# Product tiles in two pairs and a scan state in two tiles, in a fused attention and state-space kernel

## The chip, the cores and the metric

The kernel runs on one core of a Trainium2 chip as one launch. The metric is the device time of that launch in microseconds (us), less is better. TensorE (PE) multiplies matrices, ScalarE (ACT) computes exponentials, VectorE (DVE) does elementwise work, GpSimd (POOL) almost nothing, and SyncE (SP) issues the transfers.

## The reference

Two branches read one input `x` (2048 positions, 512 channels) and are mixed by a gate per position:

```python
g = _sigmoid((x * gate_w).sum(-1, keepdims=True))
a = _A_ref(x, wqkv, wo)          # softmax attention, 32 heads of 16, full 2048 x 2048 scores
b = _B_ref(x, A_re, A_im, ...)   # state-space convolution, 128 complex modes per channel
return g * a + (1 - g) * b

# in _B_ref
P = exp((dt * A)[:, :, None] * l)                 # powers of each mode, l = 0..2047
K = einsum("dn,dnl,dn->dl", Cc, P, dB).real       # one kernel of length 2048 per channel
y = causal convolution of u with K (by FFT), + u * Dskip
```

## The kernel before

**Attention.** 32 blocks (four heads by 512 queries) of 16 key quads each; a quad is four score tiles of 128 keys by 512 queries, one per head. All 2048 tiles go three at a time through 683 groups. For a group `qk` puts three tiles into one of two PSUM buffers `SC0`, `SC1`; `ex` (L909) is one exponential on ScalarE over the group, into a ring `ET`; `pv` multiplies by the values and sums in `OA`. At a block's end `norm_a`, `norm_b`, `norm_c` transpose and divide on VectorE.

**Vector sets.** Some quads are computed on VectorE instead. A set is one quad; its four tiles are spread over four consecutive groups (`SHAPE`: two tiles for ScalarE, one for VectorE). `bits` (L945) turns each tile's scores into the bit pattern of an approximate power of two in `DZ`; `batch` (L956) makes two shifted copies (`DU`, then `DZ` again), and the three versions are multiplied with the values and two scaled copies of them (`VS0`, `VS1`, made behind the groups in `VSAT`). The exponential of such a group is two tiles wide, 128x1024.

**State space.** `params` computes the modes and their powers `L1` to `L48` and the factor `MU` of one chunk of 64 positions. `base` builds the first 16 powers of each channel block in `B16`. `table` (L1211) makes the power tables: for each of 8 pairs of channel blocks it copies the 16 powers into `PT` and multiplies them by the 16th, 32nd and 48th power. Each complex product is, for its real and its imaginary part, two products into `tt1` and `tt2` and one sum into `PT`, through the helper `tt` (L1006). `PT` then goes to memory (`ptd`). `kstage` makes convolution kernels from it, `sstage` (L1297 on) the states of 32 chunks in `SG0` and `SG1` (channels 0 to 255, 256 to 511), evicted at L1309. `scan` (L1317) runs over the chunks, for each half in turn: the state `G` (fp32, real and imaginary) is multiplied by `MU` into `s2` and `s3` (L1336, L1338), the chunk's own state is added to `s2` (L1341), both are summed into `G` (L1344), and `G` is rounded to bf16 back into `SG` (L1347), 30 steps a half. The y stage multiplies states by powers, evicts 32 units (L1420), and reads them back turned; the last additions (L1575) and an output matmul of four row blocks close the kernel.

**The order of work** is computed when the kernel is built. Every operation is recorded with a cost; `Sched` holds generators with priorities (`table` 2, `scan` 3, `sstage` 2), and between two exponentials it fills the engines with whatever is ready, by start time and then priority. Each engine then runs its recorded list in order, with semaphore waits for what an operation depends on, its own engine's earlier instructions included for VectorE. An operation that would have to wait a moment for its predecessor lets another ready one go first.

Whether a set is taken is decided in `decide` (L799), group by group, inside windows:

```python
plan["used"] = max(plan["used"], idle() - DVCAP)
if plan["set"] is None and clear(x) and idle() - plan["used"] >= dvq():
    plan["used"] += dvq()
```

`idle()` is the time in which the planner's own books have VectorE idle so far; `dvq()` is the price of a set in such idle time, by `DVQ` dependent on which stage is done; credit over `DVCAP` lapses. `WIN` lists windows in groups: first, last, how many `DZ`/`DU` buffers, and how many of the two lists of key quads may be taken. `SGAT` gives the groups behind which the S stage of each half may start; `BUP` is the priority of the two steps. `place` packs all SBUF tiles by their first and last use into the free space.

Of the kernel before, what the change touches and what calls it, by code (L numbers as in the profile page):

```python
# [2 lines left out]

# [10 lines left out]
P = 128  # L14
# [21 lines left out]
BARE = 1  # L36
NS = 15
SGH = 256
SGAT = (175, 315)
SMM = .058  # L40
YR = 4
DOV = .8
# [372 lines left out]
def declare(nc, es):  # L415
# [72 lines left out]
        sb(f"B16{k}", 2 * 128 * 16)  # L488

    sb("PT", 2 * 2 * CB * T)  # L490
    sb("tt1", 2 * CB * 16)
    sb("tt2", 2 * CB * 16)
    sb("Qt", 2 * 32 * 128)
    sb("Kst", 2 * 8 * P)

    sb("SG0", 33 * 2 * SGH)
    sb("SG1", 33 * 2 * SGH)
    sb("G", 2 * 256, FP32)
    for n in ("s2", "s3"):
        sb(n, 2 * 256, FP32)  # L500

# [24 lines left out]
def place(nc, bufs):  # L526

    base, end = (nc.sbuf_base + 31) // 32 * 32, nc.sbuf_usable_end
    sbs = [b for b in bufs.values() if b.kind == "sb" and b.first is not None]

    def fit(order):
        done, top = [], base
        for b in order:
            n = (b.nbytes() + 31) // 32 * 32
            busy = sorted((o.lo, o.hi) for o in done if o.first <= b.last + 1 and b.first <= o.last + 1)
            at = base
            for lo, hi in busy:
                if at + n <= lo:
                    break
                at = max(at, hi)  # L540
            b.lo, b.hi = at, at + n
            top = max(top, b.hi)
            done.append(b)
        return top

    best, seed = None, 1
    for k in range(400):
        def rank(b):
            nonlocal seed
            seed = (seed * 1103515245 + 12345) % 2 ** 31  # L550
            w = seed / 2 ** 31 * (0 if k < 2 else .8)
            return (-(b.last - b.first > 300) if k % 2 else 0, -b.nbytes() * (1 + w * 2) * (b.last - b.first + 20) ** (w if k >= 2 else 0))
        order = sorted(sbs, key=rank)
        top = fit(order)
        if best is None or top < best[0]:
            best = (top, order)
    k = 0
    while best[0] > end and k < 12000:
        k += 1
        order = list(best[1])  # L560
        for _ in range(1 + k % 3):
            seed = (seed * 1103515245 + 12345) % 2 ** 31
            b = order.pop(seed // 7 % len(order))
            seed = (seed * 1103515245 + 12345) % 2 ** 31
            order.insert(seed // 7 % (len(order) + 1), b)
        top = fit(order)
        if top <= best[0]:
            best = (top, order)
    assert best[0] <= end, (best[0] - end, live(sbs))
    fit(best[1])  # L570
# [41 lines left out]
def record(nc, p, B, ins):  # L612
# [597 lines left out]

    def table():  # L1211
        yield ("AFTER", "D48")
        t1, t2 = B["tt1"], B["tt2"]
        H10 = dv(1024, 2)
        for pb in range(NBLK // 2):
            qr, blks = pb // 2, (2 * pb, 2 * pb + 1)
            yield ("AFTER", f"base{qr}")
            if pb:
                yield ("AFTER", f"K{2 * pb - 2}")
                yield ("AFTER", f"K{2 * pb - 1}")  # L1220
            B16 = B[f"B16{qr}"]
            bk = [(B16, 0), (B16, (1, 0)), (B16, (1, 64))]
            d0, b0 = 2 * CB * pb, 2 * CB * (pb % 2) * 16
            W = [(PT, 0, blks[0]), (PT, 1, blks[1])]
            for i in range(2):
# [3 lines left out]
            for m in range(1, 4):  # L1229
                Dm = B[f"D{16 * m}.{qr}"]  # L1230
                for part in range(2):
                    for ti, xr, yr in ((t1, 0, part), (t2, 1, 1 - part)):
                        yield ("DVE", H10)
                        tt("DVE", lambda ti=ti: ti(0, [[16, 2 * CB], [2, 8], [1, 2]]),
                           lambda xr=xr, b0=b0, B16=B16: B16(xr * 2048 + b0, [[16, 2 * CB], [2, 8], [1, 2]]),
                           lambda yr=yr, d0=d0, Dm=Dm: Dm(yr * 2 * P + 2 * (d0 % P), [[2, 2 * CB], [0, 8], [1, 2]]), ALU.mult,
                           bk + [(Dm, 0)], [(ti, 0)], H10)
                    yield ("DVE", H10)
                    tt("DVE", lambda part=part, m=m: PT(part * CB * T + 16 * m, [[PTN, 2], [T, CB], [1, 16]]),
                       lambda: t1(0, [[CB * 16, 2], [16, CB], [1, 16]]), lambda: t2(0, [[CB * 16, 2], [16, CB], [1, 16]]),  # L1240
                       ALU.add if part else ALU.subtract, [(t1, 0), (t2, 0)], W, H10)
# [73 lines left out]


    def scan():  # L1317
        G, s2, s3 = B["G"], B["s2"], B["s3"]
        MU = B["MU"]
        e = "DVE"  # L1320

        W = [[256, 2], [1, 256]]

        def pair(h):
            sg, d0 = SG[h], 256 * h
            ks = [(sg, k, (h, 'S')) for k in range(32)]
            for k in range(8):
                yield ("AFTER", f"sg{8 * h + k}")
            for c in range(NCH - 1):
                so = 2 * SGH * (c + 1)  # L1330
                if c == 0:
                    yield (e, .34)
                    op(e, lambda v, so=so: v.tensor_copy(G(0, W), sg(so, [[SGH, 2], [1, 256]])), ks, [(G, 0)], c=.34)
                    continue
                yield (e, F5)
                op(e, lambda v: v.tensor_tensor(s2(0, W), G(0, W), MU(d0, [[0, 2], [1, 256]]), ALU.mult), key("G", "MU"), [(s2, 0)], c=F5)  # L1336
                yield (e, F5)
                op(e, lambda v: v.tensor_tensor(s3(0, W), G(256, [[-256, 2], [1, 256]]), MU(D + d0, [[D, 2], [1, 256]]), ALU.mult),  # L1338
                   key("G", "MU") + [(MU, 1)], [(s3, 0)], c=F5)
                yield (e, F5)  # L1340
                op(e, lambda v, so=so: v.tensor_tensor(s2(0, W), s2(0, W), sg(so, [[SGH, 2], [1, 256]]), ALU.add),  # L1341
                   [(s2, 0)] + ks, [(s2, 0)], c=F5)
                yield (e, F5)
                op(e, lambda v: v.tensor_tensor(G(0, [[1, 512]]), s2(0, [[1, 512]]), s3(0, [[1, 512]]), ALU.add),  # L1344
                   [(s2, 0), (s3, 0)], [(G, 0)], c=F5)
                yield (e, .34)
                op(e, lambda v, so=so: v.tensor_copy(sg(so, [[SGH, 2], [1, 256]]), G(0, W)), key("G"),  # L1347
                   ks if c < NCH - 2 else [(sg, k, (h, 'G')) for k in range(32)], c=.34)
# [35 lines left out]
    def ystage():  # L1384
        def unit(u):
# [14 lines left out]
            for q in range(4):  # L1400
                yield ("PE", .15)
                for ri in range(2):
                    for j in range(4):
                        i = 4 * q + 2 * (j % 2) + j // 2
                        mm(lambda q=q, j=j: MB(64 * q, [[1, 64]], 32 * j, 32),
                           lambda ri=ri, i=i: sg(ri * SGH + CB * k8 + 16 * hf + 8 * (i % 2) + i // 2, [[2 * SGH, 32]]),
                           lambda ri=ri, i=i: Py(r * YN + ri * 16 * T + i * T, [[1, T]]),
                           [(sg, b_, (h, 'G')) for b_ in range(32)] + [(sg, "z"), (Py, r, u)], ky, False, False,
                           pos=(0, 32 * j), c=.075 if j == 0 else 0, a=16, cfg="C")
            for q in range(4):  # L1410
                yield ("PE", .09)
# [406 lines left out]
```

## Time and profile before

| | us |
|---|---|
| median of three runs | 838.77 |
| the three runs | 838.77, 840.81, 838.6 |
| span of the profiled execution, first to last instruction | 837.7 |
| ScalarE busy | 819.1 (98%) |
| VectorE busy | 783.3 (94%) |
| TensorE matmuls busy | 698.3 (83%) |
| first exponential starts, last one starts | 11.6, 827.3 |
| first scan rounding, last scan rounding | 401.3, 689.6 |

The profiled execution's own time is its span of 837.7 us; the launch's time has about 1 us more around it. Sums are made against the span and carried over to the median by that difference. In the profile's rows a group of instructions has its count, then its busy time and the mean duration of one, then the idle time of its engine just before its members. Durations of neighbours overlap on VectorE and ScalarE, so a rate is read from starts or from busy time over count, and not from the mean duration.

### The profile page before, as it was taken

To read this page: it belongs to the slowest core of one execution; us is meant where nothing else is said; L and a number is where in the kernel's file an instruction comes from. 1 tells how busy PE (TensorE), PEld (TensorE's weight loads), DVE (VectorE), ACT (ScalarE), POOL (GpSimd) and SP (SyncE) were. 2 spreads that over 40 slices of the span, in tenths; PEclk is the share of its full clock that TensorE was granted. 3 is DMA by queue.
4 is the path that set the end of the run, shared out by engine and by line. 5 is a ranking of instruction groups with operands and counts; after the bars stand their busy time and mean duration, and the time that the engine had idled before them with its cause. 6 is when DMAs were issued, how large, how long until landed. Compare 5 with 4: busy or idle time off the path is not lost.

```text
span 837.7 us, 21043 instructions
## 1 busy us (share of the span) xinstructions
PE 698.3 (83%) x8982; PEld 253.4 (30%) x8982; DVE 783.3 (94%) x1344; ACT 819.1 (98%) x695; POOL 11.0 (1%) x13
## 2 busy tenths in 40 slices
PE   7877777787679888887788887788897779999996
PEld 3232332122122332332232332244342224333332
DVE  5799999999889998999999999999899999999996
ACT  7999999999999999999999999999999999999996
POOL 4000000000000000000000000000000000000000
PEclk9999999999999999999999999999999999999999
DMA  9650044792361976873392846045564414544113
GB/s 207 142 83 10 23 77 92 202 228 57 128 177 46 223 123 179 119 205 67 139 144 40 143 67 143 1 108 136 140 148 109 115 54 110 135 99 132 34 45 101
DMA packets 248465, 94.90 MB, mean 113 GB/s; under 512 B 223156, under 2 KB 235316, under 8 KB 246324
## 3 DMA queue, kind: packets, MB, share of 16 engines
q1 hardware_dynamic: 246500, 92.51, 49.6%
q8 instruction: 70, 1.15, 0.5%
q10 hardware_dynamic: 1872, 1.05, 0.5%
q14 instruction: 23, 0.19, 0.1%
HBM read 33.08 MB, written 35.01 MB: 81 GB/s over the span
## 4 chain that ended last, share of the span: by engine, by line
ACT 83%; DVE 7%; PE 5%; DMA 3%; SPq 0%; issue 0%; ACTq 0%; DVEq 0%
ACT ET L909 83%; PE SC L628 2%; PE OA L628 2%; DVE tt L1006 2%; DMA gm_ptd<-PT 2%; DVE PT L1006 1%; DMA Wk<-in_A_wqkv_dram 1%; DVE DZ L945 1%; PE MB L628 1%; DMA XY<-gm_xrd 1%; DVE DZ L956 0%; DVE s L1336 0%; DVE OT L980 0%; DVE s L1338 0%; SPq L1371 0%
## 5 line engine op out<-in xcount | busy, mean ns | idle before, releaser
L909 ACT ACTIVATE ET<-SC 128x1536 bf16<-128x1536 f32 (+1 forms) x683 | 810.8, 1537 | 5.9 <-PE SC L628 3.6
L628 PE MATMUL SC<-Qm,KT 32*128 32x512 bf16 x2048 | 276.1, 387 | 122.4 <-ACT ET L909 107.7
L628 PE MATMUL OA<-wm 128*32 128x512 bf16 (+3 forms) x1374 | 204.1, 365 | 1.2 <-DVE wm L681 1.2
L945 DVE TENSOR_SCALAR DZ<-SC 128x512 uint16<-128x512 f32 x256 | 170.1, 684 | 10.3 <-PE SC L628 9.4
L628 PE MATMUL OA<-ET,VE 128*32 128x512 bf16 x1792 | 179.7, 394 | 0.0
L628 PEld LDWEIGHTS SC<-Qm,KT 32*128 32x128 bf16 x2048 | 70.9, 91 | 339.8 <-ACT ET L909 303.1
L628 PEld LDWEIGHTS OA<-ET,VE 128*32 128x32 bf16 x1792 | 45.7, 93 | 102.0 <-issue 97.6
L628 PEld LDWEIGHTS OA<-wm 128*32 128x32 bf16 (+2 forms) x1374 | 54.6, 95 | 25.9 <-issue 17.7
L956 DVE TENSOR_SCALAR DZ<-DZ 128x2048 uint16<-128x2048 uint16 x64 | 43.8, 684 | 3.0 <-PE OA L628 2.7
L1309 DVE TENSOR_SCALAR SG<-MB 128x512 bf16<-128x512 f32 x64 | 43.7, 684 | 3.0 <-DMA gm_ptd<-PT 1.7
L956 DVE TENSOR_SCALAR DU<-DZ 128x2048 uint16<-128x2048 uint16 x64 | 43.1, 684 | 0.1
L628 PE MATMUL MB<-X,Qt 128*128 128x64 bf16 x512 | 42.1, 244 | 1.2 <-DVE SG L1309 1.2
L1344 DVE TENSOR_TENSOR G<-s,s 128x512 f32<-128x512 f32 x60 | 41.3, 688 | 1.1
L1338 DVE TENSOR_TENSOR s<-G,MU 128x512 f32<-128x512 f32 x60 | 41.1, 684 | 0.0
L1341 DVE TENSOR_TENSOR s<-s,SG 128x512 f32<-128x512 f32 x60 | 41.0, 683 | 0.0
L1336 DVE TENSOR_TENSOR s<-G,MU 128x512 f32<-128x512 f32 x60 | 40.9, 682 | 0.0
L628 PEld LDWEIGHTS MB<-X,Qt 128*128 128x128 bf16 x512 | 28.8, 116 | 20.0 <-issue 20.0
L1006 DVE TENSOR_TENSOR ft<-FP,L 128x1024 f32<-128x1024 f32 (+1 forms) x32 | 34.4, 1086 | 0.2
L1006 DVE TENSOR_TENSOR PT<-tt,tt 128x1024 bf16<-128x1024 bf16 x48 | 32.9, 685 | 0.5
L628 PEld LDWEIGHTS MB<-Py,SG 128*32 128x32 bf16 x1024 | 27.8, 168 | 6.8 <-issue 4.1
L628 PE MATMUL MB<-Py,SG 128*32 128x64 bf16 x1024 | 28.6, 231 | 0.0
L1347 DVE CAST SG<-G 128x512 bf16<-128x512 f32 x60 | 25.3, 422 | 1.1
(167 smaller groups left out, 613.9 us busy)
## 6 DMA issues: line engine op xcount, KB each, us to landing
gm_ptd<-PT SPq DMA_DIRECT2D x16, 1024.0 KB, 5.9
Py<-gm_ptd SPq DMA_DIRECT2D x32, 512.0 KB, 4.3
gm_kpd<-Kst SPq DMA_DIRECT2D x16, 256.0 KB, 3.1
Tt<-gm_kpd SPq DMA_DIRECT2D x128, 32.0 KB, 3.2
gm_xrd<-in_A_x_dram SPq DMA_DIRECT2D x1, 2048.0 KB, 13.7
gm_xcd<-wm SPq DMA_DIRECT2D x4, 512.0 KB, 10.4
gm_xcd<-XR SPq DMA_DIRECT2D x32, 64.0 KB, 1.9
Wo<-in_A_wo_dram SPq DMA_DIRECT2D x4, 512.0 KB, 3.8
```

Source lines behind the costliest of these rows:

```text
L628: op("PE", lambda t: t.matmul(out(), lhsT(), rhs(), start=start, stop=stop, skip_group_check=True, **kw), R, W, c=c, lat=.15, a=a, cfg=cfg)
L909: op("ACT", lambda a: a.activation(ET(512 * e, [[1, 512 * n]]), sc(0, [[1, 512 * n]]), AF.Exp, scale=DH ** -0.5), [(sc, i, g) for i in ran ...
L945: op("DVE", lambda v: v.tensor_scalar(z.u16(512 * k, [[1, 512 * n]]), sc(512 * na, [[1, 512 * n]]), XS, XB, ALU.mult, ALU.add), [(sc, na + ...
L956: op("DVE", lambda v: v.tensor_scalar(t.u16(0, [[1, 2048]]), z.u16(0, [[1, 2048]]), float(STEP[k][0]), None, ALU.add), R, W, c=.07 + 2048 ...
L1006: op(eng, lambda v: v.tensor_tensor(o(), a(), b_(), f), R, W, c=c)
L1309: op("DVE", lambda v, kh=kh, part=part: v.tensor_scalar(sg(2 * SGH + SGH * part + CB * k8 + 16 * kh, [[2 * SGH, 32], [1, 16]]), MB(0, [[16 ...
L1336: op(e, lambda v: v.tensor_tensor(s2(0, W), G(0, W), MU(d0, [[0, 2], [1, 256]]), ALU.mult), key("G", "MU"), [(s2, 0)], c=F5)
L1338: op(e, lambda v: v.tensor_tensor(s3(0, W), G(256, [[-256, 2], [1, 256]]), MU(D + d0, [[D, 2], [1, 256]]), ALU.mult), key("G", "MU") + [(M ...
L1341: op(e, lambda v, so=so: v.tensor_tensor(s2(0, W), s2(0, W), sg(so, [[SGH, 2], [1, 256]]), ALU.add), [(s2, 0)] + ks, [(s2, 0)], c=F5)
L1344: op(e, lambda v: v.tensor_tensor(G(0, [[1, 512]]), s2(0, [[1, 512]]), s3(0, [[1, 512]]), ALU.add), [(s2, 0), (s3, 0)], [(G, 0)], c=F5)
L1347: op(e, lambda v, so=so: v.tensor_copy(sg(so, [[SGH, 2], [1, 256]]), G(0, W)), key("G"), ks if c < NCH - 2 else [(sg, k, (h, 'G')) for k i ...
```

## The change

The table's products go into two pairs of tiles, used in turn, and the sum of product n is issued between the two products of n + 1. The scan's state alternates between two tiles, and the rounding of a step's state is issued in the next step, between that step's second and third sums; the y stage waits for the roundings by a name of their own for each chunk. The search that packs the tiles is another one, with new random moves. Six constants of the planner change.

```diff
-SGAT = (175, 315)
+SGAT = (227, 311)
-VSAT = (158, 500)
-WIN = ((170, 475, 2, 1), (475, 540, 3, 1), (540, 678, 4, 2))
-DVQ = (("scan1", 0.0), ("scan0", 0.5), ("S15", 1.0), (None, 0.5))
+VSAT = (138, 474)
+WIN = ((184, 482, 2, 1), (482, 540, 3, 1), (540, 678, 4, 2))
+DVQ = (('scan1', 0.25), ('scan0', 0.5), ('S15', 1.25), (None, 0.5))
 BP = 2.2
-DVCAP = 2.0
-BUP = 1
+DVCAP = 5.0
+BUP = 0
...
-    sb("tt1", 2 * CB * 16)
-    sb("tt2", 2 * CB * 16)
+    for n in ("tt10", "tt11", "tt20", "tt21"):
+        sb(n, 2 * CB * 16)
...
-    sb("G", 2 * 256, FP32)
+    for n in ("G0", "G1"):
+        sb(n, 2 * 256, FP32)
...
+            def product(n, ti, xr, qr=qr, B16=B16, b0=b0, d0=d0, bk=bk):
+                m, part = 1 + n // 2, n % 2
+                Dm, t, yr = B[f"D{16 * m}.{qr}"], B[f"tt{ti}{n % 2}"], (part, 1 - part)[xr]
+                tt("DVE", lambda: t(0, [[16, 2 * CB], [2, 8], [1, 2]]),
...
+            def total(n, W=W):
+                m, part = 1 + n // 2, n % 2
+                t1, t2 = B[f"tt1{n % 2}"], B[f"tt2{n % 2}"]
+                tt("DVE", lambda: PT(part * CB * T + 16 * m, [[PTN, 2], [T, CB], [1, 16]]),
...
+            for n in range(7):
+                if n < 6:
                     yield ("DVE", H10)
+                    product(n, 1, 0)
+                if n:
+                    yield ("DVE", H10)
+                    total(n - 1)
+                if n < 6:
+                    yield ("DVE", H10)
+                    product(n, 2, 1)
...
+        def cast(h, c):
+            sg, G = SG[h], B[f"G{c % 2}"]
+            op(e, lambda v: v.tensor_copy(sg(2 * SGH * (c + 1), [[SGH, 2], [1, 256]]), G(0, W)), [(G, 0)], [(sg, ("G", c), h)], c=.34)
...
+            for c in range(1, NCH - 1):
                 so = 2 * SGH * (c + 1)
...
+                G, H = B[f"G{1 - c % 2}"], B[f"G{c % 2}"]
...
+                if c > 1:
+                    yield (e, .34)
+                    cast(h, c - 1)
                 yield (e, F5)
...
+                op(e, lambda v, H=H: v.tensor_tensor(H(0, [[1, 512]]), s2(0, [[1, 512]]), s3(0, [[1, 512]]), ALU.add),
+                   [(s2, 0), (s3, 0)], [(H, 0)], c=F5)
+            yield (e, .34)
+            cast(h, NCH - 2)
```

More of the change, by code (lines that the diff above doesn't have):

```diff
@@ L529, in place @@
     sbs = [b for b in bufs.values() if b.kind == "sb" and b.first is not None]
+    n, cap = len(sbs), end - base
+    size = [(b.nbytes() + 31) // 32 * 32 for b in sbs]
+    near = [[j for j in range(n) if j != i and sbs[j].first <= sbs[i].last + 1 and sbs[i].first <= sbs[j].last + 1] for i in range(n)]
+    rnd = random.Random(1)
     def fit(order):
[L532 to L538, printed above, removed]
-                    break
[L540 to L569, printed above, removed]
@@ L570, in place @@
-    fit(best[1])
+        at = [-1] * n
+        for i in order:
+            x = 0
+            for lo, hi in sorted((at[j], at[j] + size[j]) for j in near[i] if at[j] >= 0):
+                if x + size[i] <= lo:
+                    break
+                x = max(x, hi)
+            at[i] = x
+        return at, sum(max(0, at[i] + size[i] - cap) for i in range(n))
+    keys = (lambda i: (-size[i], sbs[i].first - sbs[i].last), lambda i: -size[i] * (sbs[i].last - sbs[i].first + 20),
+            lambda i: (sbs[i].first + 300 > sbs[i].last, -size[i]))
@@ new lines, in place @@
+    order = min((sorted(range(n), key=key) for key in keys), key=lambda o: fit(o)[1])
+    at, cost = fit(order)
+    for k in range(30000):
+        if not cost:
+            break
+        bad = [i for i in range(n) if at[i] + size[i] > cap]
+        r = rnd.random()
+        i = rnd.choice(bad) if r < .6 else rnd.choice(near[rnd.choice(bad)]) if r < .8 else rnd.randrange(n)
+        new = list(order)
+        p = new.index(i)
+        new.pop(p)
+        new.insert(rnd.randrange(p + 1) if r < .6 else rnd.randrange(n), i)
+        a, c = fit(new)
+        if c <= cost or rnd.random() < math.exp((cost - c) / (2000 * max(.02, 1 - k / 30000))):
+            order, at, cost = new, a, c
@@ L571, in place @@
+    assert not cost, (cost, live(sbs))
+    for b, x in zip(sbs, at):
+        b.lo = base + x
+        b.hi = b.lo + (b.nbytes() + 31) // 32 * 32
     for b in sbs:
@@ L1228, in table @@
                                                                      B16(b0 + i * CB * 16, [[2048, 2], [16, CB], [1, 16]])), bk, [W[i]], c=.34)
[L1229 to L1237, printed above, removed]
-                    yield ("DVE", H10)
-                    tt("DVE", lambda part=part, m=m: PT(part * CB * T + 16 * m, [[PTN, 2], [T, CB], [1, 16]]),
-                       lambda: t1(0, [[CB * 16, 2], [16, CB], [1, 16]]), lambda: t2(0, [[CB * 16, 2], [16, CB], [1, 16]]),
-                       ALU.add if part else ALU.subtract, [(t1, 0), (t2, 0)], W, H10)
+            def product(n, ti, xr, qr=qr, B16=B16, b0=b0, d0=d0, bk=bk):
+                m, part = 1 + n // 2, n % 2
+                Dm, t, yr = B[f"D{16 * m}.{qr}"], B[f"tt{ti}{n % 2}"], (part, 1 - part)[xr]
+                tt("DVE", lambda: t(0, [[16, 2 * CB], [2, 8], [1, 2]]),
+                   lambda: B16(xr * 2048 + b0, [[16, 2 * CB], [2, 8], [1, 2]]),
+                   lambda: Dm(yr * 2 * P + 2 * (d0 % P), [[2, 2 * CB], [0, 8], [1, 2]]), ALU.mult, bk + [(Dm, 0)], [(t, 0)], H10)
@@ new lines, in total @@
+            def total(n, W=W):
+                m, part = 1 + n // 2, n % 2
+                t1, t2 = B[f"tt1{n % 2}"], B[f"tt2{n % 2}"]
+                tt("DVE", lambda: PT(part * CB * T + 16 * m, [[PTN, 2], [T, CB], [1, 16]]),
+                   lambda: t1(0, [[CB * 16, 2], [16, CB], [1, 16]]), lambda: t2(0, [[CB * 16, 2], [16, CB], [1, 16]]),
+                   ALU.add if part else ALU.subtract, [(t1, 0), (t2, 0)], W, H10)
+            for n in range(7):
+                if n < 6:
+                    yield ("DVE", H10)
+                    product(n, 1, 0)
[5 more added lines that the diff above has]
+                    product(n, 2, 1)
@@ L1342, in pair @@
                    [(s2, 0)] + ks, [(s2, 0)], c=F5)
+                if c > 1:
+                    yield (e, .34)
+                    cast(h, c - 1)
                 yield (e, F5)
[L1344 to L1348, printed above, removed]
+                op(e, lambda v, H=H: v.tensor_tensor(H(0, [[1, 512]]), s2(0, [[1, 512]]), s3(0, [[1, 512]]), ALU.add),
+                   [(s2, 0), (s3, 0)], [(H, 0)], c=F5)
+            yield (e, .34)
+            cast(h, NCH - 2)
             sch.mark(f"scan{h}")
@@ L1407, in unit @@
                            lambda ri=ri, i=i: Py(r * YN + ri * 16 * T + i * T, [[1, T]]),
[L1408 removed]
+                           [(sg, ("G", c), h) for c in range(1, NCH - 1)] + [(sg, k, (h, 'S')) for k in range(32)] + [(sg, "z"), (Py, r, u)], ky, False, False,
                            pos=(0, 32 * j), c=.075 if j == 0 else 0, a=16, cfg="C")
```

16 lines of the change are left out of this document (6 added, 10 removed).

## The prediction

> **What bounds the kernel now.** The page's engine shares come first, then the ScalarE groups kept apart by shape, then busy time by stage.
>
> ```profile
> span 837.7 us, 21043 instructions
> PE 698.3 (83%) x8982; PEld 253.4 (30%) x8982; DVE 783.3 (94%) x1344; ACT 819.1 (98%) x695; POOL 11.0 (1%) x13
> ACT 83%; DVE 7%; PE 5%; DMA 3%; SPq 0%; issue 0%; ACTq 0%; DVEq 0%
> L909 ACT ACTIVATE ET<-SC 128x1536 bf16<-128x1536 f32 x426 | 582.8, 1756 | 1.9 <-PE SC L628 1.6
> L909 ACT ACTIVATE ET<-SC 128x1024 bf16<-128x1024 f32 x257 | 248.4, 1175 | 3.9 <-PE SC L628 2.0 <-PE OA L628 1.6
> 241.60:690.00 448.40, 375.46 (x4974) 136.68 (x4970) 432.73 (x754) 445.29 (x375) 1.05 (x2) 0.99 0.55 120
> 690.00:828.70 138.70, 129.12 (x2087) 50.82 (x2087) 130.05 (x223) 137.02 (x140) 0.00 (x0) 1.00 0.39 95
> 828.70:837.70 9.00, 4.24 (x24) 1.50 (x20) 3.72 (x8) 1.17 (x2) 0.00 (x0) 0.92 0.18 59
> ```
>
> ScalarE is busy for 98% of the span and holds 83% of the chain that ended last. Its 683 exponentials (426 of three score tiles, 257 of two) are the work. In the stage rows the columns are PE, weight load, DVE, ACT, POOL. ScalarE idles 1.7 us of the last full stage and the closing tail is 9.0 us. So nothing shortens this kernel unless tiles leave ScalarE or its gaps go. Tiles leave by the vector sets: a set takes four tiles of one key quad, one from each of four groups, and computes them on VectorE. The 257 short groups are 64 sets (and one group at the end). VectorE is the second engine at the limit, 94%. What the change does to VectorE therefore reaches the end only through the number of sets, and I price a set first.
>
> On ScalarE a long group occupies 582.8 / 426 = 1.37 us, a short one 248.4 / 257 = 0.97 us: a set saves 4 x 0.40 = 1.6 us. On VectorE a set is four conversions (L945) and two steps (L956). Their starts, in a stretch where nothing waits, give the price:
>
> ```profile
> 329.24 1.92 DVE L945 TENSOR_SCALAR DZ<-SC 128x512 uint16<-128x512 f32 x3
> 331.08 0.68 DVE L956 TENSOR_SCALAR DU<-DZ 128x2048 uint16<-128x2048 uint16 x1
> 331.68 0.69 DVE L945 TENSOR_SCALAR DZ<-SC 128x512 uint16<-128x512 f32 x1
> 332.29 0.68 DVE L956 TENSOR_SCALAR DZ<-DZ 128x2048 uint16<-128x2048 uint16 x1
> 332.89 0.69 DVE L956 TENSOR_SCALAR DU<-DZ 128x2048 uint16<-128x2048 uint16 x1
> ```
>
> Each lasts 0.68 us, yet the next starts 0.60 us after it: neighbours overlap by 0.08. A set costs 6 x 0.60 = 3.6 us of VectorE. So 3.6 us freed on VectorE are worth at most 1.6 us at the end, 0.44 for one.
>
> **The change, part by part.** The instruction counts stay: a table pair still has 12 products and 6 sums, a scan step still 4 sums or products and one rounding. Only order and buffers change, so the saving is in the waits between neighbours. First the scan, in a stretch where other work hardly comes between:
>
> ```profile
> 526.36 0.43 DVE L1347 CAST SG<-G 128x512 bf16<-128x512 f32 x1
> 526.70 0.69 DVE L1336 TENSOR_TENSOR s<-G,MU 128x512 f32<-128x512 f32 x1
> 527.30 0.69 DVE L1338 TENSOR_TENSOR s<-G,MU 128x512 f32<-128x512 f32 x1
> 527.90 0.69 DVE L1341 TENSOR_TENSOR s<-s,SG 128x512 f32<-128x512 f32 x1
> 528.62 0.69 DVE L1344 TENSOR_TENSOR G<-s,s 128x512 f32<-128x512 f32 x1
> 529.35 0.43 DVE L1347 CAST SG<-G 128x512 bf16<-128x512 f32 x1
> 529.69 0.68 DVE L1336 TENSOR_TENSOR s<-G,MU 128x512 f32<-128x512 f32 x1
> L1344 DVE TENSOR_TENSOR G<-s,s 128x512 f32<-128x512 f32 x60 | 41.3, 688 | 1.1
> L1347 DVE CAST SG<-G 128x512 bf16<-128x512 f32 x60 | 25.3, 422 | 1.1
> L1341 DVE TENSOR_TENSOR s<-s,SG 128x512 f32<-128x512 f32 x60 | 41.0, 683 | 0.0
> ```
>
> The products start 0.60 apart (526.70, 527.30, 527.90). The sum L1344 reads what the instruction right in front of it wrote and starts 0.72 later (528.62); the rounding L1347 reads that sum and starts 0.73 later (529.35). A dependent neighbour costs 0.12 us. L1341, which depends on the instruction two in front, has no idle time and pays nothing. Most of the 0.12 hides as lost overlap: the rows show only 0.03 to 0.04 of it as idle, so the 1.1 us before L1344 and before L1347 mean some 31 stalls each. Walking the start times gives 31 and 32; in the other steps the scheduler had put foreign work between. Saved: 63 x 0.12 = 7.6 us. But in the new order the sum of one step stands right in front of the next step's first product, which reads it. That pair was split by the rounding before. I book it at the same 32 x 0.12 = 3.8 us; its bounds are none (always split by foreign work) and 60 x 0.12 = 7.2. The scan nets 3.8 us of VectorE (0.4 to 7.6).
>
> Now the tables:
>
> ```profile
> 235.69 1.29 DVE L1006 TENSOR_TENSOR tt<-B,D32.1_154 128x1024 bf16<-128x1024 bf16 x2
> 237.01 0.69 DVE L1006 TENSOR_TENSOR PT<-tt,tt 128x1024 bf16<-128x1024 bf16 x1
> 237.74 1.29 DVE L1006 TENSOR_TENSOR tt<-B,D32.1_154 128x1024 bf16<-128x1024 bf16 x2
> L1006 DVE TENSOR_TENSOR PT<-tt,tt 128x1024 bf16<-128x1024 bf16 x48 | 32.9, 685 | 0.5
> ```
>
> Two products and a sum take 2.05 us (235.69 to 237.74) where 3 x 0.60 = 1.80 is the pace: the sum waits for the second product, and the next product waits for the sum because it overwrites what the sum reads. With two pairs of tiles and the sums one product later, no instruction depends on its neighbour. The idle 0.5 us before the 48 sums is some 14 stalls by the same 0.035; the start times give 15 there and 11 behind a sum. Saved: 26 x 0.12 = 3.1 us (at most 96 x 0.12 = 11.5, if foreign work had split none). Last in line on these stretches is then VectorE's own rate.
>
> [...]
>
> Sum for VectorE: 3.8 + 3.1 = 6.9 us. At 3.6 us a set that is 1.9 sets, and at 1.6 us a set 3.1 us off ScalarE.
>
> **What else moves.** The first S stage may start at group 227 instead of 175, the vector windows open at group 184 instead of 170. Two sets stood in the groups from 170 to 183 that no window covers now; their 7.2 us go to tables, scan or later sets, since VectorE is the shared resource: 0 in the sum, covered by queued table work. Without that cover it is 2 x 1.6 = +3.2 us. The prices of a set (idle VectorE time that the planner wants to have seen before it grants one) go from 0 to 0.25 us behind the second scan half and from 1.0 to 1.25 while the first half ends.
>
> ```profile
> L909 ACT ACTIVATE ET<-SC 128x1024 bf16<-128x1024 f32 x121 | 113.3, 1152 | 1.7 <-PE OA L628 1.6
> L945 DVE TENSOR_SCALAR DZ<-SC 128x512 uint16<-128x512 f32 x120 | 79.0, 684 | 5.9 <-PE SC L628 5.5
> ```
>
> These two are of the stage from 690 to 828.7: 120 conversions, 30 sets. At 0.25 they need 7.5 us of idle VectorE, and its row above has 138.70 - 130.05 = 8.65 us. So the price is already paid: 0; if all of it came on top, 7.5 / 3.6 = 2.1 sets fewer, +3.3 us. The larger cap on unspent credit (5.0 for 2.0) can only turn idle time into sets: from 241.6 to 690 the row shows 448.40 - 432.73 = 15.7 us idle, and a third of it would be 5.2 us, 1.5 sets, -2.3 us. I take 0, since I see no row in which credit lapsed. The second steps' priority, the earlier scaled value tiles (group 138, 474) and the packing add no instruction: 0. TensorE keeps its matmuls; two sets more add 2 x 8 matmuls (three rounds of terms for one), against an engine at 83%: 0. The tail of 9.0 us stays.
>
> Sum: span 837.7 - 3.1 = 834.6. The median of the runs, 838.8, stands 1.1 above the span, so 835.7 us.
>
> **The rivals.** *The credit eats it.* The planner grants sets for idle VectorE time, and the stalls are such idle time in its books. From 241.6 to 690 there are 34 sets at 0.5 to 1.0 us, so at least 17 us of credit against 15.7 us of idle that the row shows. If the number of sets hangs on the price and not on the work, fewer stalls mean fewer grants, other idle time takes their place, and the set count stays at 64: 838.8, within 1.5 us. For it speaks that the two numbers nearly meet; against it that the last stage grants at almost no price, and gets longer if the scan ends sooner. Chance 0.25. That the 0.12 us belongs to the kind of instruction and not to its neighbour, so that no order saves it, gives 838.8 too; L1341 without idle time against L1344 with 1.1 us, two sums of one shape, leave it 0.03. [...]
>
> *The later S stage pushes the end.* This one is slower.
>
> ```profile
> L1309 DVE TENSOR_SCALAR SG<-MB x64: 631/684/693, 267.5 to 512.6; 128x512 bf16<-128x512 f32 x64
> 267.00:378.60 111.60, 21.45 (x32) 0.98 0.80 168
> 428.00:447.00 19.00, 5.49 (x8) 1.00 0.95 128
> L1420 DVE TENSOR_TENSOR Yst<-MB,gt x32: 384/422/436, 547.6 to 807.1; 128x256 bf16<-128x256 f32 x32
> L1575 DVE TENSOR_TENSOR AR<-AR,Yl x3: 1217/1219/1221, 819.0 to 821.3; 128x2048 bf16<-128x2048 bf16 x3
> 307.20 1.53 ACT L909 ACTIVATE ET<-SC 128x1536 bf16<-128x1536 f32 x1
> ```
>
> The first half's 32 evictions (second row, of L1309 alone) end at 378; the exponential of group 227 starts at 307.2 (last row). At the fast pace of the third row (19 / 8 = 2.4 us each) they end at 307 + 77 = 384, 6 us later, which is harmless; at the pace of the second (3.5) at 419, 41 us later. The lateness is handed on through both scan halves to the last y unit (807.1) and the final additions (819.0), which must stand before the last exponential ends at 828.7: some 10 us of room. It decides from a pace of 2.5 us (389); beyond, each us costs one. At 2.65 it is 392, 4 us too late: 842.8. For it: the chain from S to output is serial, and 2.65 lies between the two measured paces. Against it: with the tables done sooner the evictions have VectorE more to themselves. Chance 0.17, with 0.03 for too few sets at the new prices (842).
>
> **How the numbers follow.** The forecast has 0.52, no change 0.28, slower 0.20. About 0.3% (2.5 us) is what a measurement of this kernel can tell from no change: faster is below 836.3, slower above 841.3. The forecast's own range is 830.3 (all bounds at once: 7.6 + 11.5 us saved, 5.3 sets, -8.5 us) to 836.3. The range over the cases runs from 830 to 842.
>
> **What would show it.** Right: in the scan the rounding stands in front of the sum with 0.60 between starts and no idle before either, and one idle gap a step is left, before the first product; no idle before the table sums; 65 to 67 sets, that is 260 to 268 short groups; ScalarE still at 98%. The credit's case: same gaps gone, 64 sets, the idle time of VectorE unchanged. The slower case: the first S evictions from 308 us on, spaced over 2.5 us, and the final additions behind 829. Wrong altogether: ScalarE's long groups wait more for TensorE (more than 1.37 us each), or the set count moves by over 5, since then the new windows and prices rule and not the stalls.

## The result, and the profile after

The changed kernel takes 831.26 us (median of six runs, 830.84 to 832.41) against 839.72 for the kernel before, run beside it (838.6 to 844.03). The ratio is 0.9902, with a 95% interval of 0.9884 to 0.992: 1% faster. The forecast was 835.7, a gain of 0.4%. The direction holds and the time lies inside the range, but the gain is over twice the size worked out.

From the page of the changed kernel, then its two shapes of exponentials by groups:

```profile
span 829.6 us, 20938 instructions
PE 694.2 (84%) x8934; PEld 252.0 (30%) x8934; DVE 784.3 (95%) x1350; ACT 815.4 (98%) x695; POOL 11.0 (1%) x13
ACT 94%; DVE 2%; DMA 1%; SPq 1%; PE 1%; issue 0%; ACTq 0%
```

```profile
L907 ACT ACTIVATE ET<-SC 128x1536 bf16<-128x1536 f32 x422 | 577.3, 1781 | 1.1 <-PE SC L626 1.1
L907 ACT ACTIVATE ET<-SC 128x1024 bf16<-128x1024 f32 x261 | 252.7, 1217 | 0.0
```

All exponentials in one group, in the kernel before and in the changed one:

```profile
L909 ACT ACTIVATE ET<-SC 128x1536 bf16<-128x1536 f32 (+1 forms) x683 | 810.8, 1537 | 5.9 <-PE SC L628 3.6 <-PE OA L628 1.6
```

```profile
L907 ACT ACTIVATE ET<-SC 128x1536 bf16<-128x1536 f32 (+1 forms) x683 | 807.1, 1566 | 1.1 <-PE SC L626 1.1
```

ScalarE's share of the chain rises from 83% to 94%. There are 261 short groups, 65 sets, one more than before. The last two fences give the account: busy and idle together fall from 816.7 to 808.2 us. Of these 8.5 us, 4 x 0.40 = 1.6 are the extra set; the idle column gives 4.8; the other 2.1 are neighbours that overlap again. So most of the gain is waits of ScalarE that went, and not tiles that left it.

A good part of such a wait shows only as lost overlap, so below it is counted otherwise. Between starts the median is 1.330 us behind a long exponential and 0.904 behind a short one in the changed kernel, 1.331 and 0.905 in the kernel before. What a start comes later than that is its wait. Their sum falls from 17.7 to 11.6 us (-6.1); with the set's 1.7 this makes the 7.8 by which the last exponential starts sooner (827.3, now 819.5). By groups: 0 to 169, 3.9 in both; 170 to 310, 3.4 to 2.0; 311 to 474, 5.6 to 2.5; from 475 on, 4.8 to 3.2.

The tables and the scan in the changed kernel, in the timeline and then by groups:

```profile
233.04 1.29 DVE L1004 TENSOR_TENSOR tt<-B,D32.2_155 128x1024 bf16<-128x1024 bf16 x2
234.24 0.69 DVE L1004 TENSOR_TENSOR PT<-tt,tt 128x1024 bf16<-128x1024 bf16 x1
234.84 0.69 DVE L1004 TENSOR_TENSOR tt<-B,D32.2_155 128x1024 bf16<-128x1024 bf16 x1
...
521.23 0.68 DVE L1352 TENSOR_TENSOR s<-s,SG 128x512 f32<-128x512 f32 x1
521.83 0.42 DVE L1334 CAST SG<-G 128x512 bf16<-128x512 f32 x1
522.17 0.69 DVE L1358 TENSOR_TENSOR G<-s,s 128x512 f32<-128x512 f32 x1
522.89 0.69 DVE L1347 TENSOR_TENSOR s<-G,MU 128x512 f32<-128x512 f32 x1
523.50 0.68 DVE L1349 TENSOR_TENSOR s<-G,MU 128x512 f32<-128x512 f32 x1
```

```profile
L1347 DVE TENSOR_TENSOR s<-G,MU 128x512 f32<-128x512 f32 x60 | 41.2, 687 | 1.2
L1358 DVE TENSOR_TENSOR G<-s,s 128x512 f32<-128x512 f32 x60 | 41.0, 683 | 0.0
L1004 DVE TENSOR_TENSOR PT<-tt,tt 128x1024 bf16<-128x1024 bf16 x48 | 33.0, 687 | 0.1
L1334 DVE CAST SG<-G 128x512 bf16<-128x512 f32 x60 | 25.2, 420 | 0.1
```

The rounding starts 0.60 behind the sum in front of it and the next sum 0.34 behind the rounding. One gap a step is left: 0.72 from 522.17 to 522.89, in front of the first product. Two table products and a sum take 1.80 us (233.04 to 234.84), not 2.05. Walking the starts, the stalls on dependent neighbours fall from 10.7 us to 4.1.

### The profile page after: what moved, and what is told of

It reads as the page before. It is cut to its first block, busy times and chain, and to the rows that moved or that the text cites. A ratio compares the mean times of both kernels' runs of the same rounds, so it can differ in the third digit from the quotient of the medians.

```text
span 829.6 us, 20938 instructions
## 1 busy us (share of the span) xinstructions
PE 694.2 (84%) x8934; PEld 252.0 (30%) x8934; DVE 784.3 (95%) x1350; ACT 815.4 (98%) x695; POOL 11.0 (1%) x13
## 4 chain that ended last, share of the span: by engine, by line
ACT 94%; DVE 2%; DMA 1%; SPq 1%; PE 1%; issue 0%; ACTq 0%
ACT ET L907 93%; DMA ldt<-in_B_log_dt_dram 1%; DMA XY<-gm_xrd 1%; SPq L1383 1%; PE SC L626 0%; DVE s L1347 0%; PE OA L626 0%; SPq L1438 0%; DVE G L1358 0%; SPq L1377 0%; DVE s L1349 0%; DVE DZ L943 0%; DVE s L1352 0%; DVE SG L1334 0%; ACT L907 0%
## 5 line engine op out<-in xcount | busy, mean ns | idle before, releaser
L626 PE MATMUL OA<-wm 128*32 128x512 bf16 (+3 forms) x1306 | 200.0, 364 | 1.2 <-DVE wm L679 1.2
L943 DVE TENSOR_SCALAR DZ<-SC 128x512 uint16<-128x512 f32 x260 | 173.2, 685 | 11.1 <-PE SC L626 9.8
L626 PE MATMUL OA<-DZ,VS 128*32 128x512 bf16 x260 | 25.6, 384 | 0.0
```

Source lines behind the costliest of these rows:

```text
L626: op("PE", lambda t: t.matmul(out(), lhsT(), rhs(), start=start, stop=stop, skip_group_check=True, **kw), R, W, c=c, lat=.15, a=a, cfg=cfg)
L943: op("DVE", lambda v: v.tensor_scalar(z.u16(512 * k, [[1, 512 * n]]), sc(512 * na, [[1, 512 * n]]), XS, XB, ALU.mult, ALU.add), [(sc, na + ...
```

## The experiments

Three theories. *Order*: the stalls that went are the gain. *Plan*: the six constants gave another order of work, and other waits. *Late transfers*: what a plan costs is set by a few transfers that come late. In the table "waits" are those of the exponentials in the profiled execution, "V" is VectorE's time waiting for transfers in its row of waits, and the clock is TensorE's mean granted one. The profiled executions of e6 and e15 were 2 us faster than their medians and that of e17 4 us slower.

| run | sets | waits | V | clock | median, us | ratio (95%) |
|---|---|---|---|---|---|---|
| before | 64 | 17.7 | 4.1 | 0.991 | 839.72 | 1 |
| after | 65 | 11.6 | 0 | 0.996 | 831.26 | 0.9902 (0.9884 to 0.992) |
| e1 old order in after's plan | 65 | 20.9 | 0 | 0.985 | 841.47 | 1.0031 (1.0008 to 1.0054) |
| e5 old rounding alone | 65 | 15.2 | 0 | 0.994 | 835.67 | 0.9961 (0.9946 to 0.9977) |
| e6 old sums alone | 65 | 15.2 | 0 | 0.996 | 837.14 | 0.9977 (0.9967 to 0.9987) |
| e2 before, new packing | 64 | 16.1 | 4.1 | 0.994 | 838.21 | 0.9993 (0.9973 to 1.0013) |
| e7 before, loads later | 64 | 16.6 | 4.5 | 0.995 | 838.75 | 0.9997 (0.9985 to 1.001) |
| e8 e7 + new sums | 64 | 17.8 | 4.3 | 0.990 | 839.76 | 1.0009 (0.9997 to 1.0022) |
| e3 before, XY early | 64 | 14.9 | 4.5 | 0.998 | 837.9 | 0.9977 (0.9958 to 0.9995) |
| e4 after, XY early | 65 | 12.1 | 0 | 0.993 | 831.79 | 0.9906 (0.9876 to 0.9935) |
| e15 after, old credit cap | 64 | 15.3 | 0 | 0.993 | 838.66 | 0.9995 (0.998 to 1.001) |
| e10, e12 after, near constants | 65, 66 | 16.4, 11.4 | 0, 0 | 0.992, 0.997 | 835.48, 831.33 | 0.9964, 0.9916 |
| e11, e16 the same | 63, 66 | 23.5, 28.6 | 9.3, 13.8 | 0.983, 0.980 | 846.78, 846.38 | 1.0091, 1.008 |
| e13, e14 before, near constants | 64, 64 | 18.2, 20.4 | 9.2, 6.0 | 0.988, 0.991 | 840.23, 844.57 | 1.0014, 1.0053 |
| e9 the same | 64 | 23.1 | 12.5 | 0.979 | 845.87 | 1.0089 (1.0069 to 1.011) |
| e17 e16, stores first | 66 | 25.2 | 7.4 | 0.979 | 840.25 | 1.0019 (1.0002 to 1.0035) |
| e18 e17, XY early | 66 | 20.0 | 7.1 | 0.987 | 839.29 | 1.0008 (0.9999 to 1.0018) |

**The order, at a fixed plan.** After's recorded order of work is kept, and only the moved instructions go back:

```diff
+    log = move_back(log, "cast", "gsum")     # each rounding right behind its own sum (e1, e5)
+    log = move_back(log, "total", "p2")      # each table sum right behind its second product (e1, e6)
```

> The changed kernel with its plan fixed (65 sets, every other instruction in its place), but with the old order put back: each rounding right behind its state's sum, each table sum right behind its second product. Theory A (the order saves VectorE time while the kernel runs, so that TensorE and ScalarE wait less): stalls of 0.12 us come back at some 50 to 60 places, 4 to 6 us of VectorE, and the time rises from 831 to 834 or 836, with the waits of the exponentials back from about 12 us to 15 or more. Theory B (the gain comes from the new plan, the order only lets the planner draw it): under 1.5 us, 831 to 832.5.

> The changed kernel, its plan fixed, with the old order in the scan alone (each rounding right behind its state's sum); the tables stay as changed. From the run with both old orders, where 13 us more of dependent waits on VectorE cost 10 us, theory A (every us of such waits costs about 0.75 at the end while the plan is fixed, wherever it lies): some 66 more waits of 0.12 us, 7.8 us, +5.9, so about 837. Rival (the loss came from few places in the tables, on which the convolution kernels wait): under +2, below 833.5.

> The changed kernel, its plan fixed, with the old order in the tables alone (each sum right behind its second product); the scan stays as changed. Theory A: 48 more waits, 5.4 us, +4.0, so about 835.3. Rival (few places in the tables): +8 or more, 839 to 841.

By the ratios, against after's 0.9902, e1 is 1.29% or 10.8 us slower, e5 5.0, e6 6.3: the two halves add up. From e1's page, and then its groups on VectorE:

```profile
ACT 57%; DVE 35%; PE 5%; issue 1%; DMA 1%; ACTq 0%; DVEq 0%
```

```profile
L1419 DVE TENSOR_TENSOR G<-s,s 128x512 f32<-128x512 f32 x60 | 41.1, 685 | 1.4
L1065 DVE TENSOR_TENSOR PT<-tt,tt 128x1024 bf16<-128x1024 bf16 x48 | 33.2, 692 | 1.7
L1395 DVE CAST SG<-G 128x512 bf16<-128x512 f32 x60 | 25.7, 428 | 2.1
```

Every rounding and every table sum now stalls, and so do 40 of the 60 state sums, since the plan, made for the new order, put nothing between: 60, 48 and 40 stalls, 17.2 us against after's 4.1. Those 13.1 us cost 10.8, some 0.8 for one, and the chain runs through VectorE for 35%. The sets can't change here, the plan being fixed, so none of this goes by way of them at 0.44: time that a plan did not count on goes into waits. e1 is slower than the 834 to 836 us expected, and it has more stalls than before itself (10.7 us), so 10.8 us is not the price of the 6.6 us that the change took out. Nor is there one price: e5's 66 more stalls (7.8 us) cost 5.0, some 0.6 for one, e6's 48 (5.4 us) cost 6.3, some 1.2.

**The same order at before's plan, and the packing.** e2 takes the new packing alone. e8 puts the new table order into before's plan. Its second pair of tiles needs room, which comes from five loads issued later; e7 has these alone and is the control. For a second state tile there was no room, so the scan's half was not tried at that plan.

```diff
+    sb("tt11", 2 * CB * 16)
+    sb("tt21", 2 * CB * 16)
...
+        if k == "total" and n % 18:   # a sum waits until the next product has been issued
+            held = (f, q, a)
```

> The kernel before with nothing but the new packing search: the same instructions in the same order, other addresses. All theories: no change, 838 to 841, within 0.3% of before. If addresses matter, over 2 us either way.

> Control for the next run: the kernel before, its plan fixed, packed by the new search, with five loads issued later on SyncE's queue (three of the S stage's four inputs for the first half, two reloads of attention rows), which makes room for two more product tiles. All theories: no change, 837 to 840, since each is still issued seven groups or more ahead of its first use.

> The control with the change's table half alone: two pairs of product tiles, each sum right behind the next product's first half. The plan, its 64 sets and all else stay. Theory A: 26 waits of 0.12 us go, 3.1 us, and at 0.75 the time falls by 2.4 us against the control, to about 836. Theory B (only a new plan can draw the gain): under 0.7 us.

Packing is worth nothing that shows. e8 against e7 is 0.0012 slower, and their intervals overlap: at before's plan the table stalls that went bought nothing, though the idle time before the sums fell from 0.5 to 0.1 us. The 2.4 us that *order* expected did not come. A wait of 0.9 us at the exponential at 244 in e7 is gone in e8; but the profiled e8 ran at a mean clock of 0.990 and the profiled e7 at 0.995, and e8's waits are 1.2 us longer in sum. The clock differs between executions of one kernel: the mean of e7's twelve goes from 0.988 to 0.997.

**One transfer.** Both kernels wait for the turned input `XY` near 594 to 602. e3 and e4 issue its load earlier.

```diff
+HOIST = [('XY1', 'pair')]     # e3: the second part of XY1's load right behind its first part, in SyncE's queue
+HOIST = [('XY1', 20)]         # e4: both parts 20 places earlier
```

> The kernel before with one transfer moved: the second half of the second input load of the y stage is issued right behind the first half, some 25 places earlier on SyncE's queue. Theory B (single late transfers that stop TensorE make up the lost ScalarE time): the three waits at 594 to 597 us (2.2 us) go, time 836 to 837. Theory A (VectorE's stalls make it up): the waits come back elsewhere, under 1 us.

> The changed kernel with both halves of that same load issued 20 places earlier. Theory B: the waits at 596 to 602 us (1.1 us) go, time 830 to 830.5. Theory A: no change.

Beside before, e3 is 1.5 us faster by the medians. But e3 has the new packing too, and beside e2, which has only that, it is 0.3 us faster by the medians and 1.0 by the means: about 1 us at most, where 2.2 us of waits were to go. After gains nothing. The rows of before show how there can be more in such a wait than the wait: TensorE's row of waits, two stretches of 3.4 us (columns PE, weight load, DVE, ACT, POOL, then the granted clock), and score matmuls in and behind the second:

```profile
PE MB L628 <- DMA XY<-gm_xrd: 1.2, 1, 1.2
```

```profile
590.50:593.90 3.40, 1.84 (x39) 0.90 (x31) 1.98 (x5) 3.28 (x3) 0.00 (x0) 1.00 0.44 65
593.90:597.30 3.40, 3.40 (x35) 0.68 (x31) 2.79 (x5) 2.05 (x2) 0.00 (x0) 0.51 0.74 195
```

```profile
595.42 0.61 PE L628 MATMUL SC<-Qm,KT 32*128 32x512 bf16 x3
...
597.85 0.39 PE L628 MATMUL SC<-Qm,KT 32*128 32x512 bf16 x3
```

TensorE stands still for 1.2 us, the next 3.4 us have half the clock, score matmuls take 0.61 instead of 0.39 us, and ScalarE is fed late: busy for 2.05 of 3.4 us. Leaving out the start and the end, such stretches fill 13.6 us of before and 6.8 of after. They are a small part of the gain: at a mean clock of 0.995 or 0.996 after takes 830.9 to 831.4 us, and before, in its runs beside the experiments, 836.5 to 839.4.

After waits as long for `XY`, from 600.15 to 601.33, but no half clock follows: in the two stretches of 3.4 us on whose border the wait lies, TensorE is busy for 2.53 and 2.87 us, and the granted clock is 1.00 in both. That fits with e4's nothing.

```profile
597.40:600.80 3.40, 2.53 (x33) 0.73 (x29) 3.40 (x8) 3.40 (x4) 0.00 (x0) 1.00 0.95 149
600.80:604.20 3.40, 2.87 (x48) 1.16 (x52) 2.30 (x8) 2.98 (x3) 0.00 (x0) 1.00 0.37 117
```

**The constants.** e15 undoes one of the six. The others move four constants a little and keep the order of before or after; all of them have the new packing.

```diff
-DVCAP = 5.0
+DVCAP = 2.0           # e15, all else as in after
...
-SGAT = (227, 311)
+SGAT = (230, 317)     # e10; e11 (224, 316), e12 (231, 308), e16 (223, 308); VSAT, WIN, DVQ as near
...
-SGAT = (175, 315)
+SGAT = (169, 320)     # e9, in before; e13 (171, 316), e14 (180, 318); VSAT, WIN, DVQ as near
```

> The kernel before, old order, old cap and step priority, with other constants near its own: S stage behind groups 169 and 320, scaled values at 152 and 502, windows from 174, 475 and 544, prices 0, 0.4, 1.0, 0.6. The planner's own books end 2.3 us earlier than for the kernel before, with the same 64 sets. Theory C (the time is that of the plan, and a plan drawn anew moves it by some us with or without the new order): 835 to 837.5, the waits of the exponentials down from 17 us by the same amount. Theory A (only the order frees VectorE): no change, 838 to 840.

> The changed kernel, new order kept, with constants a few groups and 0.1 us away from its own (S stage behind 230 and 317, scaled values at 142 and 472, windows from 186, 485 and 544, prices 0.25, 0.6, 1.35, 0.5). 65 sets as before; the planner's books end 3.2 us later. Theory C: 833.5 to 836.5, the waits of the exponentials up from 12 us by about as much. Theory A: 831 to 832, since the order and the number of sets are the same.

> The same with another near plan (S stage behind 224 and 316, scaled values at 133 and 468, windows from 185, 485 and 538, prices 0.35, 0.6, 1.25, 0.6), which takes 63 sets. The books end 3.3 us later. Sets at 1.7 us each account for 3.4 us: about 834.7, with the waits of the exponentials unchanged at some 12 us. If fewer sets relieve VectorE by 7 us, the waits fall and part of it comes back: 832.5.

> The changed kernel with a near plan whose books end 1.3 us earlier and which takes 66 sets (S stage behind 231 and 308, scaled values at 143 and 479, windows from 185, 479 and 545, prices 0.15, 0.6, 1.15, 0.4). One set more is worth 1.7 us at unchanged waits: 829.6 to 830.5, better than both kernels. If VectorE is too full for it, the waits of the exponentials rise over 13 us and the time stays at 831 to 833.

> The kernel before, old order, with a second set of near constants (S stage behind 171 and 316, scaled values at 162 and 505, windows from 173, 474 and 540, prices 0.1, 0.5, 0.9, 0.4); 64 sets. Theory C (each plan is a draw; its late transfers and half-clock stretches set the time, with either order): anywhere from 833 to 848, and the time is 838.8 plus the difference of the exponentials' waits from 17.8 us. Theory D (plans drawn for the old order lie above those for the new): 837 or more.

> The same with a third set (S stage behind 180 and 318, scaled values at 152 and 503, windows from 165, 477 and 537, prices 0.1, 0.6, 1.1, 0.5); 64 sets. Theory C: 833 to 848, by its waits. Theory D: 837 or more.

> The changed kernel with the cap on unspent credit at its old value, 2.0; all else as changed. The planner takes 64 sets. If the cap alone drew the 65th set: 1.7 us, 833.0, waits unchanged at 12 us. Theory C: the new plan's waits decide, 832 to 840. Theory D: below 837.

> The changed kernel with another near plan of 66 sets. Theory C: 828 to 836, by its waits (each us of waits above 12 adds one to 829.6). Theory D: below 837.

One constant, which the prediction booked at 0, takes the whole gain away (e15: 0.9995), by one set and 3.7 us of waits in its profiled execution. In the old order four plans give 838 to 846 us, in the new order six give 831 to 847. The fastest is new, but the two overlap: how much the new order gives on the mean of many plans these runs don't settle. The time doesn't follow the set count (66 sets: 831.3 and 846.4), it follows the waits. That is bookkeeping, since sets and waits together make up ScalarE's time; what makes the waits is the question. The planner's own books don't foretell them: they had e9 2.3 us sooner than before, and it came some 7 later; they had e11 3.3 us later than after, and it came some 15 later. VectorE's and TensorE's waits for transfers differ between the plans: here before, after, e9 and e16, one fence each.

```profile
DVE PT L1227 <- DMA gm_ptd<-PT: 2.4, 1, 2.4
DVE SG L1309 <- DMA gm_ptd<-PT: 1.7, 1, 1.7
```

```profile
PE MB L626 <- DMA XY<-gm_xrd: 1.2, 1, 1.2
```

```profile
DVE PT L1224 <- DMA gm_ptd<-PT: 7.2, 4, 2.4
DVE Qs L715 <- DMA gm_qd<-Qs: 3.5, 1, 3.5
DVE B L1003 <- DMA gm_qd<-Qs: 1.8, 1, 1.8
```

```profile
DVE PT L1224 <- DMA gm_ptd<-PT: 13.8, 4, 8.1
```

In after VectorE never waits for a transfer. Nor does it in e10 and e12, both below 836 us; in the four slowest it does for 6.0 to 13.8 us. It is no sufficient rule: e15 has none and takes 838.66, with 3.4 us of TensorE waiting for `XY`, and e13 with 9.2 us takes 840.23, less than e14 with 6.0.

**The late transfer.** e16's worst place in the timelines of VectorE, TensorE, ScalarE and SyncE, and 13.7 us of it by engine:

```profile
139.09 0.68 DVE L1004 TENSOR_TENSOR PT<-tt,tt 128x1024 bf16<-128x1024 bf16 x1
...
150.37 1.22 DVE L1004 TENSOR_TENSOR ft<-FP,L 128x1024 f32<-128x1024 f32 x1
159.68 0.43 DVE L1224 COPY PT<-B 128x1024 bf16<-128x1024 bf16 x1 [8.09 <-DMA gm_ptd<-PT]
163.96 0.68 DVE L716 CAST Qs<-MB 128x512 bf16<-128x512 f32 x1
```

```profile
164.70 1.03 PE L626 MATMUL MB<-xT,Wq 128*128 128x512 bf16 x2 [8.88 <-DVE Qs L716]
```

```profile
166.33 1.45 ACT L907 ACTIVATE ET<-SC 128x1536 bf16<-128x1536 f32 x1 [8.69 <-PE SC L626]
```

```profile
155.56 0.99 SPq L1252 DMA_DIRECT2D gm_ptd<-PT  x2
```

```profile
156.50:170.20 13.70, 5.50 (x26) 1.09 (x27) 8.21 (x15) 4.41 (x4) 0.00 (x0) 0.50 0.90 269
```

And the same store in after:

```profile
140.26 1.00 SPq L1252 DMA_DIRECT2D gm_ptd<-PT  x2
```

The table, which must be stored before `PT` is overwritten, was ready at 139.8 (139.09 + 0.68). SyncE, which runs its list in order, reached the store at 155.56, behind copies of the turned input and the attention's own transfers. VectorE stands for 8.1 us, and the next projection's eviction `Qs` stands behind it, so TensorE can't make scores: ScalarE stands for 8.7 us, and the clock is 0.50 for 13.7. In after the store is issued at 140.26, and VectorE waits for none. e17 moves those copies behind the stores, at the first four tables, and at the first one the attention's stores of `Qs` (`qd`) as well; e18 also issues `XY` 20 places earlier.

```diff
+        mv = [j for j in sp if log[j][2][3][0][0].name in (("XR", "xcd", "qd") if done == 1 else ("XR", "xcd"))]   # of the 12 SyncE entries ahead
...
+    log[last + 1:last + 1] = moved                                              # behind the table's two stores
```

> The 66-set plan that took 846.4 us, with nothing changed but SyncE's queue: copies of the turned input that stood among the 12 entries ahead of a power table's stores go behind them, so that the stores are issued some 7 to 10 us earlier. Theory 'one late transfer': the VectorE copy PT<-B at 159.7 no longer waits for DMA gm_ptd<-PT (it waited 8.1 us), the exponentials' waits at 163 to 168 (10.2 us) go, and so does most of the half clock that follows (13.7 us of it around there): 836 to 838. Rival 'too many sets for VectorE': with 66 sets and this plan VectorE is late anyhow; the waits come back within the next 30 us or at the next table, and the time stays at 843 or more.

> The same, with both halves of the second key half's turned load (XY1) also issued 20 places earlier in SyncE's queue. Theory 'one late transfer': the wait of TensorE for XY near 612 (1.9 us, and the waits behind it) goes too: another 2 to 3 us, 833.5 to 835.5; about 829 if the waits of the exponentials come down to the 12 us of the 831 us plan. Rival: the time stays within 1 us of the run with the stores alone, as the same move left the changed kernel where it was.

VectorE's rows of waits in e17, then in e18, from 140 to 200 us, and ScalarE's in e18 from 185 to 195:

```profile
DVE PT L1313 <- DMA gm_ptd<-PT: 4.8, 2, 2.9
DVE Qs L805 <- DMA gm_qd<-Qs: 2.6, 1, 2.6
```

```profile
DVE PT L1313 <- DMA gm_ptd<-PT: 5.0, 2, 3.1
DVE Qs L805 <- DMA gm_qd<-Qs: 2.1, 1, 2.1
```

```profile
ACT ET L996 <- PE SC L715: 4.6, 1, 4.6
```

Moving nothing but entries of SyncE's queue takes 6.1 us off (846.38 to 840.25; by the ratios 5.1). The 8.1 us wait is gone and so are the waits at 163 to 168: that much of e16's excess is shown to come from the order of SyncE's entries around the tables' stores. The edit acts at four tables, so the one store isn't priced alone. But the time ends between the two theories, 2 us above the first one's range. What went behind the stores comes late itself (`Qs`, 2.6 us), and the next table's store is late again (2.9 and 1.9 us, at 184 to 187), with an exponential 4.4 us late behind it (4.7 in e18). e18's `XY` wait goes as well (3.3 us of TensorE in e17, none in e18), for another 0.96 us where 2 to 3 were expected and the rival had under 1. So the late transfers carry a part of the spread; the rest of it stays open.

## Why the prediction was right and wrong

**The stalls: right.** 6.9 us were to go, 6.6 went. The order in the traces is the one foretold, down to the one gap left in a step, where 34 neighbours stall against 32 booked. A dependent neighbour costs 0.12 us in both kernels (0.72 us from start to start, against 0.60).

**From VectorE to the end: the step that failed.** "What the change does to VectorE therefore reaches the end only through the number of sets", 6.9 us for 1.9 sets and 3.1 us. One set came, 1.7 us. The waits of the exponentials, not in the sum, fell by 6.1 us. The text allowed for gaps ("unless tiles leave ScalarE or its gaps go"), but read them from the idle column, 5.8 us in its two groups; measured from starts they were 17.7. And the chain quoted there had 15% in VectorE, TensorE and DMA, which it passed over. How far from 0.44 the price can lie, e1 and e8 show: 0.8 for one at after's plan, through waits alone, and nothing at before's. The set's own price was right: 1.6 us booked, 1.7 found. What lowered the waits, the order or the constants, is not separated: in after's plan the old order takes the whole gain away (e1), and so does one old constant with the new order (e15).

**The constants: wrong at 0.** They add no work, but a changed one can give another plan, and e15 prices one at 7.8 us. The item's lower bound, -2.3, was short as well. The packing at 0 holds (e2). The 1.1 us from span to median mixes two executions: in every run on record the launch takes 1.8 to 2.2 us more than its own span.

**The rivals.** The credit didn't eat it in this plan, yet e15 with the old cap has 64 sets and 838.66, what that rival gave: with the stalls gone, at a cap of 2.0 the grants are as few as before. That the order doesn't matter is refuted by e1, 10.8 us slower at the same plan. In before and after, a product or sum of the scan that reads its neighbour's result starts 0.72 us behind it, one that doesn't 0.60.

The later S stage came, and its condition was met, and it did no harm. In the changed kernel: all evictions, the roundings and the last additions by line, and the last eviction of the first half in the timeline.

```profile
L1317 DVE TENSOR_SCALAR SG<-MB x64: 653/686/695, 306.8 to 516.0; 128x512 bf16<-128x512 f32 x64
L1334 DVE CAST SG<-G x60: 385/421/464, 430.1 to 677.6; 128x512 bf16<-128x512 f32 x60
L1587 DVE TENSOR_TENSOR AR<-AR,Yl x3: 1170/1227/1229, 814.0 to 816.8; 128x2048 bf16<-128x2048 bf16 x3
```

```profile
410.23 0.69 DVE L1317 TENSOR_SCALAR SG<-MB 128x512 bf16<-128x512 f32 x1
```

(410.23 - 306.8) / 31 = 3.34 us for an eviction, well over the 2.5 from which it should have decided, and 26 us later than the 384 that was harmless. But the lateness wasn't handed on: the first rounding is 29 us later than before (401.3) and the last one 12 us earlier (689.6). The scan took 247.5 us instead of 288.3. The tables, ahead of the S stage now, were done sooner (last copy into `PT` at 340, before at 374); that this left VectorE to the scan is likely, but no run isolates it. (At 2.5 us an eviction the first half would end at 387, not at the 389 of that rival, which changes nothing.) The additions still lie in front of the end.

**The range.** "Wrong altogether" was to be a set count that moves by over 5, or long groups over 1.37 us. Neither came: 577.3 / 422 is 1.37. Yet the plan did rule, by waits that the set count doesn't show.

## What to carry to other kernels

Price the bounding engine's gaps by its starts against its free pace, not by an idle column, which showed a third of them in the kernel before and a tenth in the changed one. Where a planner or a scheduler makes the order, a change to its constants is a change to every wait; it has a spread of its own (15 us here, against a gain of 8), which one before and one after can't tell from the change itself. So hold the order fixed and move single instructions, as e1 and e17 do, before naming a cause.

## What the hardware showed that was not expected

In before, without start and end, the granted clock fell to half for 3.4 us twice and for 6.8 once, in after for 3.4 twice, and in e16 for 13.7. Behind before's 3.4 us from 590.50 it fell although TensorE had no longer wait in them than 1.2 us; it was busy for 1.84. In front of the other falls in before TensorE was busy for 2.55 and 2.06 of 3.4 us (from 180.9 and 317.5), in after for 2.14 and 2.19 (from 184.4 and 201.5). The busy time of the 3.4 us in front alone does not tell a fall from none: in after it was 2.13 from 239.0 and 2.10 from 669.1, and the clock stayed full behind both. What decides is not shown.

A wait of 1.2 us for a transfer can thus cost twice, as in before: once as itself, and again by the slow matmuls behind it (0.61 us for a score matmul instead of 0.39). It need not, as after shows. And in e16 SyncE's queue, whose list runs in order, held a finished table back for 16 us (139.8 to 155.56).
